# One written order for units 16 to 127, seven products from unit 20 on, and a new plan for the first batch

## The chip, the cores and the metric

The kernel runs on one core of one Trainium2 chip. The core has five engines that matter here, and the rows of the profile name them so: PE (TensorE, with PEld for its weight loads), DVE (VectorE), ACT (ScalarE), POOL (GpSimd) and SP (SyncE, which here only issues DMAs). The metric is the device time of one execution in microseconds (us); lower is better.

## The reference

An attention with a few global tokens, then a two-layer network with a leaky activation:

```python
# batch 8, heads 8, local length 512, global length 32, head size 64, window 32
s_ll = scale * q_l @ k_l^T, masked to |i - j| <= 32
a_l  = softmax(concat[scale * q_l @ k_g^T, s_ll])
out_l = a_l @ concat[v_g, v_l]
out_g = softmax(scale * q_g @ concat[k_g, k_l]^T) @ concat[v_g, v_l]
x = concat[out_g, out_l] as (8 * 544, 512)
h = x @ w_in                      # 512 x 2048
g = max(h, 0) + alpha * min(h, 0) # alpha per hidden column
return g @ w_out                  # 2048 x 512
```

All of it is fp32.

## The kernel before, in words

**Units.** The network is cut into 144 units. Unit T = 16 G + f takes token group G (groups 0 to 7 are the 512 local tokens of a batch, group 8 all 256 global tokens) and hidden block f of 128 columns. A unit has a first layer (`f1`, tile `h_ps`), the activation (tiles `g`, then `gh` and `gl`), and a second layer (`f2`, tiles `o0` to `o3`, shown as `o`) that adds into four banks over the 16 units of a group. The second layer of a unit runs LAG = 2 units after its first layer.

**Three matmuls for one.** An fp32 number is held as an upper part of fewer bits and the rest (`xh` and `xl`, `gh` and `gl`, two halves of `wt`). A product of two such numbers takes three matmuls: upper by upper, rest of the weight by upper, upper by rest. A plain first layer of a unit is so 4 x 3 = 12 matmuls of 512 columns, and a second layer 12 more.

**Seven products.** `f1_fast` takes the first layers of two units (an even one and the odd one after it) together, as a 2 x 2 matrix of blocks by the seven-product scheme. Each product is 6 matmuls of 256 columns: four products (24 matmuls) in the even unit and three (18) in the odd one, 42 against the 24 of 512 columns that two plain first layers take. It needs sums of weights (`weight_sums(q)` for pair q of hidden blocks, tiles `wsum`, `s24`, `s3`), sums of x (`x_sums`, tiles named `b11` to `t4`) and, behind the products, five additions on VectorE (tiles `u` and `h_ps`).

**Activation.** `prelu` is two VectorE instructions that read `h_ps`. The other form, `negatives` on ScalarE and then `add_slopes` on VectorE, has one. In the seven-product units the last pair of a group uses the second form (functions `added` and `both`), the others the first (`even` and `odd`).

**Attention.** It goes in pairs P = 0 to 31 of two heads (four per batch): scores (`s_ps`), softmax, global scores (`g_ps`), values (`o_ps`). The probabilities of P >= 4 go through DRAM to be transposed (`scratch`, `pt`). The pairs of batch G + 1 run in the units of batch G, four units to a pair.

**What sets the order.** Units 0 to 15, with the decoding of all 32 weight tiles (`wraw`, `wt`, `wr`) and attention pairs 0 to 8, stand in an order that the class `Plan` makes in `begin`: each operation has an engine, a cost, its needs and a due time, and `LIST` holds the numbers, with a bias per kind of operation. Its names are `S`, `G`, `T`, `V` (scores, global scores, transposes, values of a pair), `fx`, `fy`, `f1` (first layer of a unit, units 0 and 1 in parts), `fa` and `fb` (second layer by `gh` and by `gl`), `red` (the reduction of scores), `p` (activation), `su` and `d1` to `d3` (weight decoding). Units 16 to 29 (`slow_unit`) are plain, and a list scheduler orders all engines but TensorE there; TensorE runs in the order of the program everywhere. Units 30 and 31 (`border_units`) and 32 to 127 (`fast_unit`, set by `FAST`) stand as written. Units 16, 23 and 30 (`CATCH`) hold two attention steps instead of one. Weight sums are made in units 18 to 29 for q = 0 to 6 and in 33 and 35 for q = 7. SyncE's DMAs are put in order by the list scheduler behind `begin`.

## Time and profile before

| what | value |
|---|---|
| three runs | 884.85, 886.47, 890.36 us (median 886.47) |
| the profiled execution, its own time | 887.61 us |
| its span (first to last instruction) | 885.8 us |
| PE, share of the span | 98% |
| DVE | 70% |
| ACT | 44% |
| POOL | 37% |

The time of an execution is its span and what lies around it, here 1.8 us. A share is a mean over stages with different limits: the first 150 us are not like the rest.

### The profile page before, as it was taken

What the parts mean: (1) busy time and instruction counts of PE and PEld (TensorE: products, weight loads), DVE (VectorE), ACT (ScalarE), POOL (GpSimd) and SP (SyncE); (2) the same over time, 40 slices, a digit from 0 to 9 for tenths busy, and PEclk for the clock granted to TensorE, in tenths of its full rate; (3) what the DMA queues carried; (4) which work ended last, traced back from release to release, by engine and by line L of the source; (5) the groups of instructions that cost most, each with busy time, mean ns of one, the idle gap of its engine ahead of it and who ended that gap; (6) DMA issues with size and microseconds to landing.
All of it is one profiled execution on the core that took longest, in us unless ns stands there. A gap on an engine that the chain in (4) does not pass through costs nothing.

```text
span 885.8 us, 22467 instructions
## 1 busy us (share of the span) xinstructions
PE 866.2 (98%) x8678; PEld 751.2 (85%) x8678; DVE 616.3 (70%) x1690; ACT 392.7 (44%) x1162; POOL 323.9 (37%) x281
## 2 busy tenths in 40 slices
PE   7799999999999999999999999999999999999998
PEld 5677777878888888888898888888898898889898
DVE  7999999976767667666676667666676656455432
ACT  7898885544444334432354334432354324211221
POOL 4455443655434332423243332423243323222222
PEclk9999999999999999999999999999999999999999
DMA  9879997977457766776657666776657553645630
GB/s 357 343 256 387 335 336 251 324 247 236 152 180 220 250 214 220 263 241 232 211 173 254 211 215 217 255 250 231 212 184 250 173 185 95 215 168 169 220 134 25
DMA packets 80906, 201.23 MB, mean 227 GB/s; under 512 B 21280, under 2 KB 41248, under 8 KB 77088
## 3 DMA queue, kind: packets, MB, share of 16 engines
q1 hardware_dynamic: 80800, 199.80, 66.1%
q8 instruction: 69, 1.13, 0.5%
q14 instruction: 37, 0.30, 0.1%
HBM read 160.96 MB, written 38.80 MB: 226 GB/s over the span
## 4 chain that ended last, share of the span: by engine, by line
PE 73%; DVE 14%; DMA 6%; ACT 4%; issue 2%; POOL 1%; SPq 1%; DVEq 0%; ACTq 0%; POOLq 0%
PE o L323 34%; PE h_ps L323 30%; PE o_ps L323 4%; PE s_ps L323 3%; DVE wt L294 2%; PE g_ps L323 2%; DVE wsum L294 2%; DVE p L294 2%; DVE g L294 2%; ACT p L294 2%; DVE wraw L294 1%; DMA pt<-scratch 1%; DMA scratch<-p 1%; DMA v<-in_v_dram 1%; DMA wa<-wt 1%
## 5 line engine op out<-in xcount | busy, mean ns | idle before, releaser
L294 POOL TENSOR_TENSOR gl<-g,gh 128x512 fp32r<-128x512 f32 (+1 forms) x128 | 161.4, 1263 | 368.0 <-ACT gh L294 270.4
L323 PE MATMUL o<-gh,wo 128*128 128x512 f32 (+1 forms) x1024 | 244.4, 380 | 0.0
L323 PE MATMUL h_ps<-xh,wt 128*128 128x256 f32 (+1 forms) x1024 | 222.4, 310 | 2.2 <-DVE g L294 1.3
L294 ACT CAST gh<-g 128x512 fp32r<-128x512 f32 (+1 forms) x144 | 85.9, 597 | 289.0 <-DVE g L294 288.3
L323 PEld LDWEIGHTS o<-gh,wo 128*128 128x128 f32 x1024 | 176.7, 188 | 32.1 <-issue 0.4
L323 PEld LDWEIGHTS h_ps<-xh,wt 128*128 128x128 f32 x1024 | 166.2, 188 | 20.5 <-issue 4.0
L323 PE MATMUL h_ps<-xl,wt 128*128 128x256 f32 (+1 forms) x512 | 157.4, 307 | 0.0
L323 PE MATMUL o<-gl,wo 128*128 128x512 f32 (+1 forms) x512 | 131.2, 377 | 0.0
L294 DVE TENSOR_SCALAR g<-h_ps,alpha_sb 128x512 f32<-128x512 f32 (+1 forms) x116 | 82.5, 712 | 39.0 <-PE h_ps L323 33.6
L323 PEld LDWEIGHTS o<-gl,wo 128*128 128x128 f32 x512 | 92.8, 188 | 18.5
L294 POOL TENSOR_TENSOR p<-p,rz 128x512 f32<-128x512 f32 x64 | 70.7, 1121 | 96.2 <-DVE rz L294 93.4
L323 PEld LDWEIGHTS h_ps<-xl,wt 128*128 128x128 f32 x512 | 96.1, 188 | 5.1
L294 DVE TENSOR_TENSOR h_ps<-u,h_ps 128x256 f32<-128x256 f32 x144 | 61.1, 425 | 50.6 <-PE h_ps L323 48.7
L294 ACT ACTIVATE p<-p,mn 128x128 f32<-128x128 f32 x224 | 86.9, 396 | 5.1 <-DVE mn L294 4.9
L323 PE MATMUL h_ps<-xh,s 128*128 128x256 f32 x480 | 88.6, 280 | 0.4 <-DVE h_ps L294 0.2
L294 DVE TENSOR_TENSOR u<-u,h_ps 128x256 f32<-128x256 f32 x96 | 40.3, 420 | 57.0 <-PE h_ps L323 36.7
L323 PEld LDWEIGHTS h_ps<-xh,s 128*128 128x128 f32 x480 | 75.9, 188 | 4.3 <-ACT xe L294 0.7
L294 DVE SCALAR_TENSOR_TENSOR g<-h_ps,g 128x512 f32<-128x512 f32 (+1 forms) x116 | 75.9, 654 | 3.8
L323 PE MATMUL h_ps<-xl,s 128*128 128x256 f32 x240 | 67.1, 279 | 0.0
L294 POOL TENSOR_TENSOR wt<-wt,wr 128x512 int32<-128x512 int32 x32 | 45.4, 1423 | 52.4 <-DVE wt L294 35.0
L323 PEld LDWEIGHTS o_ps<-pt,v 128*64 128x64 f32 x1600 | 49.7, 138 | 8.2 <-issue 2.7
L323 PE MATMUL o_ps<-pt,v 128*64 128x32 f32 (+1 forms) x1600 | 53.5, 223 | 1.7 <-DMA pt<-scratch 1.0
(102 smaller groups left out, 1137.1 us busy)
## 6 DMA issues: line engine op xcount, KB each, us to landing
wo<-wo SPq DMA_DIRECT2D x128, 512.0 KB, 4.3
v<-in_v_dram SPq DMA_DIRECT2D x29, 1024.0 KB, 5.4
qk<-in_qk_dram SPq DMA_DIRECT2D x30, 672.0 KB, 7.0
wraw<-in_w_dram SPq DMA_DIRECT2D x32, 512.0 KB, 8.4
scratch<-p SPq DMA_DIRECT2D x112, 128.0 KB, 2.8
pt<-scratch SPq DMA_DIRECT2D x28, 512.0 KB, 5.7
wo<-wt SPq DMA_DIRECT2D x16, 512.0 KB, 7.1
out_dram<-ost SPq DMA_DIRECT2D x32, 256.0 KB, 3.5
```

The source lines that it names most:

```text
L294: ins = op(*a, **k)
L323: ins = nc.tensor.matmul(*a, **k)
```

## The change

The plan of the first batch gets other numbers: other biases and due times in `LIST`, other first free times of the engines, and TensorE's costs without the 3% that were added (1.25 times up to 27 us in place of 45 us, then 1.0). What it plans is the same set of operations. All units from 16 to 127 go through one function, `unit`, and stand in the order in which they are written; `slow_unit`, `border_units`, `attn`, the double steps and `x_last` are gone. Units 16 to 19 have plain first layers with the `negatives` form (`f1_plain`), and `f1_fast` begins with unit 20 in place of unit 32. Batch 1 takes its x sums from `x_second`, batches 2 to 7 from `x_sums`. Batches 1 and 2 use `added` and `both` in all pairs. Weight sums for q = 2 to 7 stand in units 17 to 28, in two parts each, those for q = 0 and 1 in units 33 to 38; in batch 2 the hidden blocks start at 4 and wrap round (`hidden`), so that blocks 0 to 3 come last there. Attention step s of pair P stands in unit t with t + 20 = 4 P + s (before, from unit 31 on: t + 22).

```diff
 LIST = dict(
-    first=29.416, pace=6.054, pair0=79.515, pair=19.51, slack=2, ...
+    first=29.07, pace=6.054, pair0=88.993, pair=19.315, slack=2, ...
...
-FAST = range(2 * NF, NB * NF)
-CATCH = (16, 23, 30)
+PLAIN = NF + 4
+FIRSTS = {17: 2, 19: 3, 21: 4, 23: 5, 25: 6, 27: 7, 33: 0, 37: 1}
+RESTS = {18: 2, 20: 3, 22: 4, 24: 5, 26: 6, 28: 7, 34: 0, 38: 1}
...
+LATE = 4
...
-        free = dict(PE=5.4, ACT=2.5, DVE=5.0, POOL=4.0, SP=1.2)
-        lock, dma, kind, landed = 0.0, 3.3, None, [0.0] * 8
+        free = dict(PE=4.5, ACT=2.5, DVE=4.2, POOL=3.2, SP=0.7)
+        lock, dma, kind, landed = 0.0, 2.4, None, [0.0] * 8
...
-                cost = cost * (1.25 if t < 45 else 1.03) + (0.15 if kind != o["kind"] else 0.0)
+                cost = cost * (1.25 if t < 27 else 1.0) + (0.12 if kind != o["kind"] else 0.0)
...
+    def x_second(step):
+
+        if step == 0:
+            less(b11, b12, b11)
+            less(b12, b22, b12)
+            upper(1, "t1", b11)
+            upper(1, "t3", b12)
+        if step == 1:
+            xs[1, "b11"], xs[1, "b21"], xs[1, "b22"], xs[1, "t4"] = halves(0, 0), halves(2, 0), halves(2, 1), halves(0, 1)
+            lower(1, "t1", b11, vec)
+            less(b11, b22, b11)
+            upper(1, "t2", b11)
+            lower(1, "t3", b12, vec)
+            less(b21, b21, b11)
+            lower(1, "t2", b11, vec)
+        if step == 2:
+            for c in range(2):
+                act.copy(xs[1, "t4"](0, c), x_raw[:, 2 + c, 0:256])
+                pool.tensor_tensor(xs[1, "t4"](1, c), x_raw[:, 2 + c, 0:256], xs[1, "t4"](0, c).bitcast(F32), op=ALU.subtract)
...
+    def hidden(T):
+
+        G, f = divmod(T, NF)
+        return (f + LATE) % NF if G == 2 else f
...
-        if f == NF - 1:
+        if f == NF - 1 or G in (1, 2):
             return added, both
         return even, odd
+
+    def f1_plain(T):
+        h = f1(T, True)
+
+        def half():
+            us["below"] = negatives(h)
+
+        def whole():
+            g = us.pop("below")
+            add_slopes(T, g, h)
+            upper_g(T, g, SL)
+            lower_g(T, g, SL)
+
+        return half, whole
...
-    def fast_unit(t):
-        P, s = divmod(steps[t][0], 4)
+    def unit(t):
+        P, s = divmod(t + 20, 4)
...
-        one, two = f1_fast(t)
+        one, two = f1_plain(t) if t < PLAIN else f1_fast(t)
...
+            if t in FIRSTS:
+                late[FIRSTS[t]] = weight_sums(FIRSTS[t], True)
...
+        if t in RESTS and s == 2:
+            late.pop(RESTS[t])()
...
-        pin[0] = t in FAST or t in (2 * NF - 2, 2 * NF - 1)
+        pin[0] = t < NB * NF
```

The first place is TensorE in the first batch, where the second layer begins. `s_ps` are the scores of attention pair 5 (`S5`), the `h_ps` ahead of it end the first layer of unit 2, `gh` and `gl` are the activation of unit 0. Before:

```order
L323 MATMUL h_ps<-xh,wt 128x512 x2
L323 MATMUL h_ps<-xl,wt 128x512
L323 MATMUL s_ps<-qk 32x128 x32
L323 MATMUL o_1003<-gh,wt 128x512 x2
L323 MATMUL o_1004<-gh,wt 128x512 x2
L323 MATMUL o_1005<-gh,wt 128x512 x2
L323 MATMUL o_1006<-gh,wt 128x512 x2
L323 MATMUL h_ps<-xh,wt 128x512 x2
```

Now:

```order
L322 MATMUL h_ps<-xl,wt 128x512
L322 MATMUL o_942<-gh,wt 128x512 x2
L322 MATMUL o_943<-gh,wt 128x512 x2
L322 MATMUL o_944<-gh,wt 128x512 x2
L322 MATMUL o_945<-gh,wt 128x512 x2
L626 MATMUL pt<-consts,sg_sb 128x128 x3
L322 MATMUL o_942<-gl,wt 128x512
L322 MATMUL o_943<-gl,wt 128x512
L322 MATMUL o_944<-gl,wt 128x512
L322 MATMUL o_945<-gl,wt 128x512
L322 MATMUL s_ps<-qk 32x128 x32
```

Second-layer work moved ahead of the scores of pair 5. Further on, the second layer of one unit more, or its `fa` or `fb` part, stands ahead of the values of pairs 4 to 6 (`V4` now follows `fb2`, before `fb1`) and `fa` of one unit more ahead of the first layers of units 9 to 12; ahead of unit 14 and between `V7` and `G8` there is less (`V7 fb11 G8` in place of `V7 fa12 G8`). Ahead of `S4` one quarter of unit 1's first layer (`fy1`, three matmuls) came in, and on VectorE `p0` now stands between the two halves of pair 4's reduction (`red4.0`, `red4.1`) instead of behind both.

The second place is TensorE at units 20 and 21 of batch 1 (the numbers tell the buffers apart: `h_ps_2665` and `h_ps_2666` are the two banks of one pair). Before, unit 20:

```order
L323 MATMUL h_ps_2713<-xh_1235,wt_1210 128x512 x2
L323 MATMUL h_ps_2713<-xl_1236,wt_1210 128x512
L323 MATMUL h_ps_2713<-xh_1553,wt_1210 128x512 x2
L323 MATMUL h_ps_2713<-xl_1554,wt_1210 128x512
L323 MATMUL h_ps_2713<-xh_1871,wt_1210 128x512 x2
L323 MATMUL h_ps_2713<-xl_1872,wt_1210 128x512
L323 MATMUL h_ps_2713<-xh_2209,wt_1210 128x512 x2
L323 MATMUL h_ps_2713<-xl_2210,wt_1210 128x512
```

Now, the last three of its four products:

```order
L322 MATMUL h_ps_2665<-xh_2379,wt_1199 128x256 x2
L322 MATMUL h_ps_2665<-xl_2380,wt_1199 128x256
L322 MATMUL h_ps_2665<-xh_2379,wt_1199 128x256 x2
L322 MATMUL h_ps_2665<-xl_2380,wt_1199 128x256
L322 MATMUL h_ps_2666<-xh_2427,s24_2567 128x256 x2
L322 MATMUL h_ps_2666<-xl_2428,s24_2567 128x256
L322 MATMUL h_ps_2666<-xh_2427,s24_2567 128x256 x2
L322 MATMUL h_ps_2666<-xl_2428,s24_2567 128x256
L322 MATMUL h_ps_2666<-xh_2382,s3_2568 128x256 x2
L322 MATMUL h_ps_2666<-xl_2383,s3_2568 128x256
```

The plain first layer of 512 columns became half-width products, which take both banks and read weight sums (`s24`, `s3`) and x sums.

The third place is VectorE in units 16 to 18. `g` with `alpha_sb` or `beta_sb` is the activation, `x_raw` and `xl` without `o_ps` are the x sums, `gm`, `gz`, `p`, `rz` and `x_glb` belong to attention. Before:

```order
L294 TENSOR_SCALAR g<-h_ps,alpha_sb 128x512
L294 TENSOR_TENSOR wsum<-wt 128x512 x2
L294 SCALAR_TENSOR_TENSOR g<-h_ps,g 128x512
L294 RECIPROCAL rz<-rz 128x4 x2
L294 TENSOR_TENSOR wsum<-wsum 128x256 x4
L294 STREAM_TRANSPOSE p<-p 128x512 x2
```

Now:

```order
L293 SCALAR_TENSOR_TENSOR g<-g,beta_sb,h_ps 128x512
L293 TENSOR_TENSOR x_raw<-x_raw 128x2x256 x2
L293 RECIPROCAL rz<-rz 128x4 x2
L293 SCALAR_TENSOR_TENSOR g<-g,beta_sb,h_ps 128x512
L293 TENSOR_TENSOR xl<-x_raw,xh 128x512
L293 TENSOR_TENSOR x_raw<-x_raw 128x2x256
L293 TENSOR_TENSOR xl<-x_raw,xh 128x512
L293 TENSOR_TENSOR x_raw<-x_raw 128x2x256
L293 TENSOR_TENSOR xl<-x_raw,xh 128x512
L293 STREAM_TRANSPOSE p<-p 128x512 x2
L293 TENSOR_TENSOR wsum<-wt 128x512 x2
```

The activation has one VectorE instruction for two, the sums of x came in, and the weight sums moved behind them.

## Rows read from the trace of the kernel before

**Rows 1.** The page: the span, and busy time, share and number of instructions of each engine.

```profile
span 885.8 us, 22467 instructions
...
PE 866.2 (98%) x8678; PEld 751.2 (85%) x8678; DVE 616.3 (70%) x1690; ACT 392.7 (44%) x1162; POOL 323.9 (37%) x281
```

**Rows 2.** Stretches of the span: its bounds and length, then busy time and number of instructions of PE, PEld, DVE, ACT and POOL, the granted PE clock, the DMA engines' busy share and GB/s.

```profile
0.00:20.00 20.00, 15.52 (x349) 10.48 (x349) 14.90 (x58) 13.85 (x62) 10.06 (x23) 1.00 0.92 352
20.00:35.00 15.00, 10.57 (x185) 8.75 (x186) 14.24 (x46) 13.16 (x39) 9.09 (x9) 1.00 1.02 416
35.00:60.00 25.00, 22.71 (x274) 17.57 (x273) 23.85 (x74) 21.27 (x53) 10.76 (x8) 1.00 0.68 230
60.00:90.00 30.00, 28.99 (x301) 22.99 (x300) 29.24 (x82) 26.78 (x75) 16.58 (x12) 1.00 0.96 363
90.00:151.44 61.44, 59.03 (x547) 45.88 (x543) 60.05 (x152) 46.78 (x114) 27.23 (x21) 1.00 0.89 311
151.44:180.00 28.56, 28.56 (x246) 23.25 (x242) 28.15 (x63) 13.07 (x40) 16.96 (x15) 1.00 0.93 332
180.00:297.00 117.00, 115.88 (x1160) 96.71 (x1159) 81.89 (x251) 50.71 (x168) 52.13 (x46) 1.00 0.66 213
297.00:720.00 423.00, 423.00 (x4465) 376.16 (x4464) 285.09 (x830) 170.47 (x541) 137.79 (x110) 1.00 0.67 222
```

**Rows 3.** The chain of work that ended last, in order of time: start, length, what. Plain units (before 230 us) and seven-product units (from 299 us).

```profile
204.43 2.75 PE o L323 x12
207.17 2.75 PE h_ps L323 x12
...
299.90 2.12 PE h_ps L323 x18
302.02 2.75 PE o L323 x12
304.76 2.82 PE h_ps L323 x24
```

**Rows 4.** TensorE in order of time in the first batch, the instructions that waited: start, length, line, operation, tiles, shape, count, and in brackets the idle time before and what ended it.

```profile
41.56 0.38 PE L323 MATMUL s_ps<-qk 64*32 64x128 f32 x2 [1.05 <-DVE xl L294]
42.41 1.13 PE L323 MATMUL s_ps<-qk 64*32 64x128 f32 x62 [0.48 <-DVE xl L294]
...
46.90 0.73 PE L323 MATMUL h_ps<-xh,wt 128*128 128x512 f32 x2 [0.76 <-DVE g L294]
...
63.42 1.59 PE L323 MATMUL o_ps<-pt,v 128*64 128x32 f32 x48 [1.01 <-DMA pt<-scratch]
...
96.94 0.50 PE L323 MATMUL h_ps<-xh,wt 128*128 128x512 f32 x1 [0.70 <-DVE wt L294]
...
118.87 0.50 PE L323 MATMUL h_ps<-xh,wt 128*128 128x512 f32 x1 [0.20 <-DVE wt L294]
...
136.77 0.70 PE L323 MATMUL g_ps<-qk 128*64 128x288 f32 x6 [0.48 <-ACT x_raw L294]
```

**Rows 5.** The same view where batch 2 begins and where the last attention pair is done.

```profile
284.02 0.69 PE L323 MATMUL g_ps<-pt,v 128*64 128x32 f32 x16 [0.69 <-DVE g_ps L294]
...
745.22 0.48 PE L323 MATMUL h_ps<-xh,s 128*128 128x256 f32 x2 [0.25 <-DVE h_ps L294]
```

**Rows 6.** VectorE in order of time at 46 us: the last piece of the reduction of a pair's scores, and the activation of unit 0 behind it.

```profile
45.86 0.31 DVE L294 CUSTOM_DVE_ANT_0 p<-s_ps,mask 128x128 f32<-128x128 f32 x1
...
46.07 0.77 DVE L294 SCALAR_TENSOR_TENSOR g<-g,beta_sb,h_ps 128x512 f32<-128x512 f32 x1
```

**Rows 7.** All engines in order of time where unit 47, the last of batch 2, ends: the two additions into the banks, the ScalarE part of the activation, its VectorE part, and the first matmul of unit 48.

```profile
351.17 0.41 DVE L294 TENSOR_TENSOR h_ps<-u,h_ps 128x256 f32<-128x256 f32 x1
...
351.61 0.60 ACT L294 ACTIVATE g<-h_ps 128x512 f32<-128x512 f32 x1 [1.07 <-DVE h_ps L294]
351.64 2.00 PE L323 MATMUL o<-gh,wo 128*128 128x512 f32 x8
351.84 0.43 DVE L294 TENSOR_TENSOR h_ps<-u,h_ps 128x256 f32<-128x256 f32 x1 [0.26 <-PE h_ps L323]
...
352.78 1.40 DVE L294 SCALAR_TENSOR_TENSOR g<-g,beta_sb,h_ps 128x512 f32<-128x512 f32 x2
...
354.39 0.40 PE L323 MATMUL h_ps<-xh,wt 128*128 128x256 f32 x2
```

**Rows 8.** VectorE's instructions by group and shape from 300 to 640 us: count, busy us and mean ns of one, idle time before.

```profile
L294 DVE TENSOR_SCALAR g<-h_ps,alpha_sb 128x512 f32<-128x512 f32 x49 | 36.8, 751 | 2.7
L294 DVE TENSOR_TENSOR h_ps<-u,h_ps 128x256 f32<-128x256 f32 x83 | 35.3, 425 | 20.4 <-PE h_ps L323 19.3
L294 DVE SCALAR_TENSOR_TENSOR g<-h_ps,g 128x512 f32<-128x512 f32 x49 | 33.9, 692 | 1.7
...
L294 DVE SCALAR_TENSOR_TENSOR g<-g,beta_sb,h_ps 128x512 f32<-128x512 f32 x6 | 4.2, 741 | 0.0
```

**Rows 9.** Weight sums on VectorE in order of time, and GpSimd at the same time.

```profile
156.49 1.35 DVE L294 TENSOR_TENSOR wsum<-wsum 128x256 f32<-128x256 f32 x3
...
161.92 4.17 DVE L294 TENSOR_TENSOR wsum<-wsum 128x256 f32<-128x256 f32 x4
...
162.01 2.37 POOL L294 TENSOR_TENSOR p<-p,rz 128x512 f32<-128x512 f32 x2 [0.16 <-DVE rz L294]
164.35 1.46 POOL L294 TENSOR_TENSOR gl<-g,gh 128x512 fp32r<-128x512 f32 x1
```

More of the change, by code (lines that the diff above doesn't have):

```diff
@@ L794, in prepare @@
             G += 1
-        if G == NB - 1 and (f, at) in LAST_STEPS:
-            x_last(LAST_STEPS.index((f, at)))
-        if G * NF not in FAST or (f, at) not in X_STEPS:
-            return
-        if G < NB - 1:
+        if 2 <= G < NB and (f, at) in X_STEPS:
             x_sums(G, X_STEPS.index((f, at)))
@@ L827, in product @@
             for j, e in ((0, 0), (1, 0), (0, 1)):
-                matmul(dst, w[:, j, 128 * c : 128 * c + 128], x[e][:, 256 * c : 256 * c + 256], start=start, stop=not start, skip_group_check=True)
+                piece = x(e, c) if callable(x) else x[e][:, 256 * c : 256 * c + 256]
+                matmul(dst, w[:, j, 128 * c : 128 * c + 128], piece, start=start, stop=not start, skip_group_check=True)
                 start = False
+    def hidden(T):
+        G, f = divmod(T, NF)
+        return (f + LATE) % NF if G == 2 else f
     def f1_fast(T):
         G, f = divmod(T, NF)
-        q = f // 2
+        q = hidden(T) // 2
         x = lambda name: xs[G, name]
@@ L892, in add_slopes @@
     def add_slopes(T, g, h):
-        f = T % NF
+        f = hidden(T)
         vec.scalar_tensor_tensor(g, g, beta_sb[:, f : f + 1], h, op0=ALU.mult, op1=ALU.add)
@@ L903, in slopes @@
     def slopes(T, h, n):
-        f = T % NF
+        f = hidden(T)
         g = stage("g")
@@ L977, in longformer_ffn @@
     gpart = {}
-    def values(P, first):
-        last = gpart.pop(P)
-        if live(P - 1):
-            ob = bank(first, "o_ps")
-            pv_all(P - 1, ob, last)
-        if live(P):
-            global_scores(P)
-        if live(P - 1):
-            pv_out(P - 1, ob, last)
     def values_pe(P):
@@ L1151, in longformer_ffn @@
-    tails = []
     begin()
     pin_sync[0] = False
-    steps = [[] for t in range(NT + LAG)]
-    u = NPRE + NF
-    for t in range(NF, NT + LAG):
-        steps[t] = [u, u + 1] if t in CATCH else [u]
-        u = steps[t][-1] + 1
-    def attention(t, at):
-        with tc.high_priority(offset=HP):
-            if len(steps[t]) == 1:
-                attn(steps[t][0], at)
-                return
-            order = [(k, a) for k in range(2) for a in ("pre", "mid", "post")]
-            i = 2 * ("pre", "mid", "post").index(at)
-            for k, a in order[i : i + 2]:
-                attn(steps[t][k], a)
@@ L1236, in fast_unit @@
             two()
+            if t == NF:
+                x_second(0)
+            if t == PLAIN:
+                x_second(2)
+            if t in RESTS and s == 0:
+                late.pop(RESTS[t])()
             prepare(t, "mid")
@@ L1264, in fast_unit @@
         f2(t - LAG, 1)
+        if t in RESTS and s == 2:
+            late.pop(RESTS[t])()
+    late = {}
     load_out_weights(NF)
```

164 lines of the change are left out of this document (29 added, 135 removed).

## The prediction

> **What bounds the kernel now.** I read the page first, then the stretches, then the chain, then the waits of the stretch that is not full. The page says that PE is busy 98% of the span and no other engine over 70% (VectorE; PEld is TensorE's own weight load) [rows 1]. The stretches say where the other 2% are [rows 2]. From 297 to 720 us PE is busy 423.0 of 423.0 us: nothing but less matmul work makes this part shorter. From 151.44 (where the second layer of unit 14 begins) to 297 it is idle 1.1 us in 145.6, though VectorE has 35.5 us free there. Before 151.44 it is idle 14.6 us: 4.5 up to 20 us, 4.4 up to 35, 2.3 up to 60, 1.0 up to 90, 2.4 after. In that first stretch TensorE does not stand alone: from 60 to 151.44 VectorE is busy 89.3 of 91.4 us, from 35 to 60 23.9 of 25. So the first batch has two full engines, and whatever is won on TensorE there by order has to be paid out of 3.3 us of free VectorE time between 35 and 151 us. The granted clock is 1.00 in every stretch, the higher of the two levels (2.4 GHz), so no term comes from it.
>
> **The change, part by part.** The sum goes against the profiled execution, 887.61 us, which is 1.1 above the median of the three runs; I take the 1.1 off at the end.
>
> *Seven products for units 20 to 31.* The chain has the lengths of whole first layers [rows 3]. A plain one is 12 matmuls in 2.75 us, so a pair takes 5.50. With seven products the even unit is 24 matmuls in 2.82 and the odd one 18 in 2.12, together 4.94. That is 0.56 less per pair, on an engine that has no gap there; six pairs more are changed: -3.3 us (3.36). The attention work and the second layers of batches 1 to 7 stay the same in number.
>
> The Trainium skill has a rule against this term: "TensorE: Matmul & The Clock Gate", section "Back-to-back issue gap", gives about 81 ns per matmul of 128 columns and 131 ns for 512 in a stream with weight loads. An estimate between these for 256 columns is 98 ns; a pair would then be 24 x 131 = 3.1 us plain and 42 x 98 = 4.1 us with seven products, and the change would cost 1 us per pair, 5.8 in all. The trace disagrees on both: 2.75 / 12 = 229 ns and 2.12 / 18 = 118 ns [rows 3]. The measurement decides.
>
> *What the seven products ask of the others.* VectorE's price per pair goes by its own rows [rows 8]: before, two plain units took 2 x (0.75 + 0.69) = 2.9 us; now 5 x 0.43 + 2 x 0.74 = 3.6. The x sums of batch 1 come in addition, seven instructions in units 16 and 17, and nothing reads them before unit 20, over 16 us of matmuls later (three units of 5.5). Against this, the plain units 16 to 19 and all of batch 2 use the form with one VectorE instruction. The ScalarE part of that form falls on an engine that is busy 64 of 145.6 us there [rows 2]. I cost all of this at nothing, because VectorE has 35.5 us free in the stretch that takes it; if it comes in the wrong order it costs waits, which is the rival below.
>
> The one place where this form could stop TensorE is the release of the banks between two pairs. It exists already in unit 47, the last of its batch [rows 7]: the first layer ends at 351.64, the VectorE part begins at 352.78, its first half frees the first bank at 353.48, and unit 48 begins at 354.39 with no wait. The slack is 0.9 us, without scores between the pairs.
>
> *Stalls after the first batch.* Those of before are 1.1 us (to 297) and 0.25 at 745.22, where the last x sums are made [rows 2, 5]. The waits for scores and values at the change of schemes go with the old units 30 to 35; the last attention pair comes two units later and the last x sums go through the common function. New waits can come at units 20, 24 and 28, whose weight sums are finished only two units ahead. Bounds: -1.4 and, from the worst old single wait of 0.69 at each of these three and at the end of batch 6, +2.8. I take -0.5, nearer to the old state, since VectorE is no fuller than it was.
>
> *The first batch.* No operation is added or removed; only the order changes. I go through the waits that I can name [rows 4]. `S4` waits 1.05 + 0.48 us for VectorE; `fy1`, three matmuls, 0.69 us by a plain quarter, now fills part: -0.69. Unit 2's first layer waits 0.76 for `p0`, which stood behind the whole reduction of pair 4 [rows 6]; four of its eight pieces, 0.21 us apart, now come after it: -0.76. `V4` waits 1.01 for the fetch of the probabilities; a whole second layer (2.75) more stands ahead: -1.01. Units 9 and 12 wait 0.70 and 0.20 for weights; an upper half (1.83 us, 8 of 12 matmuls of 2.75) more stands ahead of each: -0.90. Against these, `G8` waits 0.48 for a copy behind `V7` with 1.83 us of cover, and now has 0.92: +0.9. Together -2.5. Earlier, up to 35 us, the order on TensorE is nearly the old one (`G1` moved ahead of `S2`, `G4` ahead of `Tg3`), and ScalarE is busy 27 of 35 us [rows 2]; I take 0 there. VectorE gives part of the gain back, since it is full from 60 us on: what TensorE no longer waits for in one place it will ask for sooner in the next. I take -2.0. Bounds: the gain ends at the 10.1 us that PE is idle between 20 and 151.44, or, with VectorE's 3.3 us as the limit after 35, at 4.4 + 3.3 = 7.7; the loss, if the order is worse where I see nothing, at the same named waits a second time, 4.7 with that of `G8`.
>
> *With one answer.* Which hidden block comes when in batch 2, the order of the stores of weights (the same DMAs of the same size, on SyncE, whose order behind the first batch is still found by the scheduler), the new first free times: they change no engine's work, and I cost them at 0. Where they need cover it is TensorE's queue of two units; DMA is busy 0.66 of the time from 180 to 297 and 0.93 before that, so a late output weight could show only between 151 and 180.
>
> Sum: 887.61 - 3.3 - 0.5 - 2.0 = 881.8 for the profiled execution, and 880.7 for the median of runs like the three shown: 0.65% less.
>
> **The rivals.**
>
> *VectorE is the limit of the first batch, and the order wins nothing there.* For it: 89.3 of 91.4 us busy. Against it: the waits named above are in TensorE's own queue, and some (the fetch) are not VectorE's. It leaves the term of the products alone: 887.6 - 3.3 - 0.5 = 883.8, median 882.7.
>
> *The order wins much more.* For it: 8.9 us of idle TensorE before 35 us, which I valued at 0. Against it: ScalarE and VectorE are nearly as full there. With the 7.7 us of the bound: 887.6 - 3.3 - 0.5 - 7.7 = 876.1, median 875.0.
>
> *Slower: the written order puts VectorE's sums ahead of what TensorE waits for.* VectorE takes its instructions in order, and now the scheduler no longer moves weight sums out of the way. A weight sum is six instructions with both inputs in SBUF. Three of them took 1.35 us alone, and four took 4.17 beside GpSimd's work of 162.01 to 165.81 [rows 9], so 0.59 more each and 3.5 for six. Queued behind it are the additions into the banks, and the next pair on TensorE waits for these. With 0.9 us of slack taken off, 2.6 remain; eight weight sums, six in batch 1 and two in batch 2, make 21 at most. With half of that, 10.5, the time is 892.3, median 891.2. It decides from 0.7 us per sum beyond the slack (5.8 / 8); below that the kernel still gains. Against it: the same contention stood in batch 1 before, and PE was idle 0.0 us from 151 to 180 beside it. The Trainium skill ("SBUF — State Buffer", section "SBUF: two separate sides") says that such a VectorE instruction and a GpSimd one hold the shared ports one at a time, the whole instruction long; the trace agrees with 4.17 against 1.8 us.
>
> *Half-width matmuls are not half as long in batch 1*, so that the change doesn't do what it says. They would have to take 5.50 / 42 = 131 ns and not 118 to win nothing. PEld is busy 376 of 423 us where they run now, so weight loads have 11% left [rows 2], and the same weights and shapes are used. It would give 885.1, median 884.0.
>
> **How the numbers follow.** Chances: my forecast 0.63 (own range 877.5 to 884), VectorE as the limit 0.18, much more 0.10, slower 0.07, no shorter products 0.02. The range goes from 875.5, past most of the second rival, to 887, past the first and the last, and leaves out the slower one and the end of the large gain. A measurement of this kernel can tell about 1% from no change, 8.9 us of 886.5, so the bounds are 877.6 and 895.3. Faster by over 1%: 0.10 and 0.08 of my own case, 0.18. Slower by over 1%: only the upper part of the slower rival, whose middle is 891.2, and what I have not thought of, 0.05. Within 1%: 0.77.
>
> **What would show it.** Right: `h_ps` groups of 24 and 18 matmuls of 256 columns from unit 20 on, 2.82 and 2.12 us long; two units of batch 1 without attention in 10.4 us (4.94 and twice 2.75) instead of 11.0; the second layer of unit 14 beginning some 2 us before 151.4; PE idle under 1.5 us from there to the end of the attention. Wrong: a first batch that is as long as before, waits of `h_ps` for VectorE at the even units 20 to 46, or waits of `o` for the load of `wo` between 150 and 190 us.

## The result, and the profile after

The change makes the kernel 0.7% slower. The changed kernel takes 893.34 us (median of 8 runs, 890.67 to 894.70), the kernel before 886.81 us beside it (8 runs); the ratio is 1.0069, 95% interval 1.0052 to 1.0087. I had forecast 880.7 us with a range up to 887.0. The profiled execution took 891.17 us, with a span of 889.4 us, 3.6 more than before [rows 1].

The stretches of the changed kernel, with columns as in [rows 2]; the first begins where the second layer of unit 14 does:

```profile
149.97:180.00 30.03, 27.52 (x242) 22.59 (x241) 21.33 (x67) 15.67 (x46) 11.02 (x9) 0.94 0.75 269
180.00:270.00 90.00, 86.81 (x894) 76.33 (x892) 69.70 (x186) 49.76 (x148) 46.44 (x41) 1.00 0.57 189
270.00:297.00 27.00, 27.00 (x320) 24.02 (x317) 17.46 (x53) 12.69 (x38) 10.23 (x9) 1.00 0.70 241
297.00:720.00 423.00, 419.61 (x4466) 371.27 (x4466) 282.23 (x841) 175.57 (x554) 137.09 (x113) 1.00 0.66 222
```

The part that had been full, 297 to 720 us, now has 3.4 us of idle TensorE; the part from 150 to 270 us has 5.7, and there the granted clock is below 1.00 for the first time. What TensorE waited for, in total, times and longest, from 149 to 297 us and from 297 to 720 us:

```profile
PE g_ps L322 <- DVE g_ps L293: 4.6, 4, 2.5
PE h_ps L322 <- POOL xl L293: 0.8, 1, 0.8
PE h_ps L322 <- DVE g L293: 0.3, 1, 0.3
...
PE h_ps L322 <- POOL xl L293: 3.4, 4, 0.9
```

Neither of these two waits is on my list. **The first** stands in the values blocks of units 18, 22, 26 and 30. TensorE and then VectorE in order of time in unit 18 of the changed kernel:

```profile
161.06 1.59 PE L322 MATMUL o_ps<-pt,v 128*64 128x32 f32 x48
165.16 0.80 PE L322 MATMUL g_ps<-pt,v 128*64 128x32 f32 x16 [2.51 <-DVE g_ps L293]
...
166.84 3.09 PE L322 MATMUL o<-gh,wo 128*128 128x512 f32 x8
...
161.33 0.68 DVE L293 TENSOR_TENSOR x_raw<-x_raw 128x512 f32<-128x512 f32 x1
161.94 0.68 DVE L293 TENSOR_TENSOR xl<-x_raw,xh 128x512 fp32r<-128x512 f32 x1
162.54 1.29 DVE L293 STREAM_TRANSPOSE p<-p 128x512 f32<-128x512 f32 x2
163.76 1.25 DVE L293 TENSOR_TENSOR wsum<-wt 128x512 f32<-128x512 f32 x2
164.97 0.72 DVE L293 SCALAR_TENSOR_TENSOR g<-g,beta_sb,h_ps 128x512 f32<-128x512 f32 x1
165.02 0.09 DVE L293 MEMSET g_ps<- 64x32 f32 x1
```

TensorE needs a bank of which VectorE first has to clear a part (0.09 us). The clearing reads nothing, but it stands behind the x sums, the transposes and the weight sums of unit 17; in units 22 and 26 it stands behind weight sums of 2.4 us, in unit 30 behind x sums of 2.3 us. From 165 to 170 us the granted clock is 0.66, a mean of the two levels (1.00 is 2.4 GHz, 0.50 is 1.2): the eight matmuls behind the wait take 3.09 us, not 2.00.

**The second** stands at the first odd unit of batches 2 to 7. Rows of all engines, in order of time, from the border of batch 4 (units 64 and 65) of the changed kernel; those between them are left out:

```profile
460.01 0.68 DVE L293 TENSOR_TENSOR xl<-x_raw,xh 128x512 fp32r<-128x512 f32 x1
460.65 0.40 PE L322 MATMUL h_ps<-xh,s 128*128 128x256 f32 x2
460.73 0.69 DVE L293 TENSOR_TENSOR x_raw<-x_raw 128x512 f32<-128x512 f32 x1
461.45 0.62 ACT L293 CAST xh<-x_raw 128x512 fp32r<-128x512 f32 x1 [0.62 <-DVE x_raw L293]
462.15 1.27 POOL L293 TENSOR_TENSOR xl<-x_raw,xh 128x512 fp32r<-128x512 f32 x1 [2.58 <-ACT xh L293]
463.48 0.38 PE L322 MATMUL h_ps<-xl,wt 128*128 128x256 f32 x1 [0.84 <-POOL xl L293]
464.04 0.39 PE L322 MATMUL o<-gh,wo 128*128 128x512 f32 x1
```

This first layer takes 464.04 - 460.65 = 3.39 us where 2.12 was the price [rows 3]. It reads the x sum t4, which goes from VectorE over ScalarE to GpSimd only now. Over the six borders this is 7.2 us (1.35, 1.33, 1.26, 1.28, 1.33, 0.68).

The same border in the kernel before (the first layer of the even unit begins, GpSimd makes t4's lower half, the first layer of the odd unit begins), and behind the dots the start of the even unit's first layer in the changed kernel:

```profile
453.96 0.40 PE L323 MATMUL h_ps<-xh,wt 128*128 128x256 f32 x2
460.73 1.29 POOL L294 TENSOR_TENSOR xl<-x_raw,xh 128x512 fp32r<-128x512 f32 x1 [2.28 <-ACT xh L294]
462.24 0.40 PE L323 MATMUL h_ps<-xh,s 128*128 128x256 f32 x2
...
454.96 0.51 PE L322 MATMUL h_ps<-xh,wt 128*128 128x256 f32 x2
```

Counted from the start of the even unit's first layer, t4 is done after 8.1 us there (462.02) and after 8.5 here (463.42): hardly later. But the odd unit's first layer begins after 8.3 us there and after 5.7 here. The values block of 2.5 us that lay between the two first layers is gone from this place; scores ahead of the even unit have come instead.

The sum from the two traces, from the start of the second layer of unit 14 to that of unit 128: 691.2 us before, 696.2 after, so + 5.0 behind a first batch that ends 1.5 us sooner (149.97, not 151.44). In it: the borders + 7.2; the g_ps waits 4.6, and 1.7 for the matmuls at the low clock (the values block from 165.16 on 1.68 us, not 1.10, the second layer behind it 3.84, not 2.75); the rest, with the seven products, is 8.5 less.

### The profile page after: what moved, and what is told of

It reads as the page before. It is cut to its first block, busy times and chain, and to the rows that moved or that the text cites. A ratio compares the mean times of both kernels' runs of the same rounds, so it can differ in the third digit from the quotient of the medians.

```text
span 889.4 us, 22789 instructions
## 1 busy us (share of the span) xinstructions
PE 863.4 (97%) x8786; PEld 752.5 (85%) x8786; DVE 614.3 (69%) x1703; ACT 414.4 (47%) x1203; POOL 321.8 (36%) x283
## 4 chain that ended last, share of the span: by engine, by line
PE 69%; DVE 12%; issue 7%; POOL 5%; DMA 3%; ACT 3%; SPq 0%; POOLq 0%; DVEq 0%; ACTq 0%
PE o L322 32%; PE h_ps L322 28%; PE o_ps L322 3%; PE s_ps L322 3%; PE g_ps L322 3%; DVE wt L293 2%; POOL gl L293 2%; DVE g L293 2%; DVE p L293 2%; POOL xl L293 2%; DVE wraw L293 1%; DMA scratch<-p 1%; DVE xl L293 1%; DVE mn L293 1%; DMA wa<-wt 1%
## 5 line engine op out<-in xcount | busy, mean ns | idle before, releaser
L322 PE MATMUL h_ps<-xh,wt 128*128 128x256 f32 (+1 forms) x1024 | 210.4, 300 | 4.2 <-DVE g L293 2.7
L322 PE MATMUL h_ps<-xl,wt 128*128 128x256 f32 (+1 forms) x512 | 152.0, 297 | 4.7 <-POOL xl L293 4.7
L293 DVE TENSOR_TENSOR h_ps<-u,h_ps 128x256 f32<-128x256 f32 x162 | 68.0, 425 | 58.4 <-PE h_ps L322 56.2
L322 PE MATMUL h_ps<-xh,s 128*128 128x256 f32 x552 | 100.1, 278 | 0.0
L322 PEld LDWEIGHTS h_ps<-xh,s 128*128 128x128 f32 x552 | 87.0, 188 | 3.8
L293 DVE TENSOR_SCALAR g<-h_ps,alpha_sb 128x512 f32<-128x512 f32 (+1 forms) x86 | 60.3, 702 | 35.5 <-PE h_ps L322 31.7
L293 DVE TENSOR_TENSOR u<-u,h_ps 128x256 f32<-128x256 f32 x108 | 45.3, 420 | 55.2 <-PE h_ps L322 51.6
L322 PE MATMUL h_ps<-xl,s 128*128 128x256 f32 x276 | 76.6, 278 | 0.0
L293 DVE CUSTOM_DVE_ANT_0 p<-s_ps,mask 128x128 f32<-128x128 f32 x224 | 49.7, 284 | 14.1 <-PE s_ps L322 12.1
L293 DVE SCALAR_TENSOR_TENSOR g<-h_ps,g 128x512 f32<-128x512 f32 (+1 forms) x86 | 55.2, 642 | 3.0
```

Source lines behind the costliest of these rows:

```text
L293: ins = op(*a, **k)
L322: ins = nc.tensor.matmul(*a, **k)
```

## The experiments

Each run stood beside the kernel before on the same chip, and ratios are to that; not all runs were on one chip. My theory (A): two waits, each the result of an order on VectorE. The rival (B): batch 1 and the borders have more VectorE work than fits, and whatever is moved, something else is late.

**Clearing g_ps one unit earlier.**

```diff
-        if s == 2 and (live(P) or live(P - 1)):
+        if s == 1 and (live(P) or live(P - 1)):
             gpart[P] = global_bank(P)
```

> The changed kernel, with one thing moved: the clearing of the bank of the global scores (g_ps, 0.09 us on VectorE) is written one unit earlier, at the start of the odd unit with s = 1, ahead of that unit's x sums and weight sums. In the trace of the changed kernel the values blocks of units 18, 22, 26 and 30 wait 4.6 us in all for this clearing, which stands in VectorE's order behind weight sums and x sums; in the first of them (2.51 us) TensorE's granted clock falls, and the second layer behind it takes 3.84 instead of 2.75 us. Theory A (the wait is only one of order): the waits of g_ps go, the clock stays at 1.00, and the time falls by 4.6 + 1.1 = 5.7, from 893.3 to about 887.6; the waits at the starts of batches 2 to 7 stay. Rival B (VectorE has too much work in batch 1, the order matters little): TensorE then waits about as long for the next thing that VectorE is late with, the additions into the banks and the slopes of batch 1, and the time stays within 1.5 us of 893.3.

Measured: 890.57 us (886.51 to 893.69), ratio 1.0055 (1.0034 to 1.0076). The median lies between the two expectations, 2.8 us under the changed kernel's on another chip. The trace, which is of the fastest of the six executions, is clear: no wait of g_ps is left behind unit 14, the clock is 1.00, and units 14 to 30 take 102.5 us, not 107.5, though one wait of 1.4 us at unit 30 is new. From the second layer of unit 14 to that of unit 128 it is 690.5 us, not 696.2: the 5.7 of theory A. The pair of runs that differ only in this edit on one chip, further down, gives 1.0065 to 1.0006, 5.2 us. Theory A for this wait; why the median here shows only half of it is open.

**The second layer ahead at the borders.**

```diff
+        border = f == 1 and t > 2 * NF
+        if border:
+            f2(t - LAG, 0)
         one, two = f1_plain(t) if t < PLAIN else f1_fast(t)
...
-        f2(t - LAG, 0)
+        if not border:
+            f2(t - LAG, 0)
```

> The changed kernel, with another order on TensorE alone at six places: in units 33, 49, 65, 81, 97 and 113 (the first odd unit of batches 2 to 7) the upper eight matmuls of the second layer that follows (1.83 us) are placed ahead of the first layer of the unit, whose last product reads the x sum t4. In the trace of the changed kernel this first layer takes 3.4 us instead of 2.1 in five of these units and 2.8 in the sixth, 7.2 us in all, with waits for the lower half of t4 on GpSimd. Theory A (t4 comes late since the unit before it now holds scores and no values block): 1.83 us of cover is more than the 1.3 us that are missing, so all of it goes, and the time falls by about 7, from 893.3 to 886.2. Rival B (the sum of many small waits of VectorE is the cause, and the border only one place where they show): PE is then idle elsewhere in the same batch, in the next pair that waits for a bank, and the time falls by less than 2 us.

Measured: 892.90 us, ratio 1.0089 (1.0076 to 1.0102): nothing won, as the rival said. VectorE and TensorE behind the first layer of unit 49 in this run:

```profile
365.51 0.43 DVE L293 TENSOR_TENSOR h_ps<-u,h_ps 128x256 f32<-128x256 f32 x1 [2.49 <-PE h_ps L322]
365.97 0.75 DVE L293 TENSOR_SCALAR g<-h_ps,alpha_sb 128x512 f32<-128x512 f32 x1
366.76 0.69 DVE L293 SCALAR_TENSOR_TENSOR g<-h_ps,g 128x512 f32<-128x512 f32 x1
...
367.60 0.47 PE L322 MATMUL h_ps<-xh,wt 128*128 128x256 f32 x2 [0.49 <-DVE g L293]
```

The first layer now takes 2.12 us, but the next pair waits for its banks, which VectorE frees in 1.9 us at the earliest, and the 1.83 us of matmuls that covered this have gone ahead. It waits for the second bank too, and takes 3.4 us instead of 2.9. The cover can be used once.

**Both.**

> Both edits: the clearing of g_ps one unit earlier, and the eight upper matmuls ahead of the first layer at the six borders. Theory A (two separate waits, both of order): the gains add up, 893.3 - 5.7 - 7.2 = 880.4, which would be faster than the kernel before by 6.4 us (0.7%), of which 3.4 are the seven products and 1.5 the first batch. Rival B (VectorE's work as such): 890 or more.

Measured: 887.50 us, ratio 1.0022 (1.0011 to 1.0032), between the two expectations. Its profiled execution has the span of the clearing alone, 884.7 us, and the borders take as long in sum as ever; that its median is 3 us lower than that of the clearing alone, whose runs spread over 7 us, I can't explain.

**The plan of the first batch alone, in the kernel before.** Its biases, due times, costs and first free times; no code.

> The kernel before, with the changed kernel's plan of the first batch alone: its biases and due times, its costs and its first free times; the units from 16 on are those of before. If the new plan by itself wins what the two traces show (the second layer of unit 14 begins 1.5 us earlier), the time is 886.8 - 1.5 = 885.3. If the gain comes from how the first batch meets units 16 and on, or is given back there, it is 886.8 or more. Had my prediction's term been right, it would be 884.8.

Measured: 886.92 us, ratio 1.0016 (1.0004 to 1.0027): 1.4 us slower, not 2.0 faster. TensorE in that trace, and the stretch behind (columns as above):

```profile
148.83 0.73 PE L323 MATMUL h_ps<-xh,wt 128*128 128x512 f32 x2 [1.90 <-DVE g L294]
...
150.00:155.00 5.00, 5.00 (x75) 3.69 (x74) 5.00 (x9) 1.14 (x2) 0.50 (x1) 0.69 1.05 382
```

Late in the batch TensorE waits 1.90 us for the slopes of a unit on VectorE, and the clock falls behind it too. The second layer of unit 14 begins at 154.5 us in this trace, 3 us later than before.

**The changed kernel once more.**

> The changed kernel itself, unedited, as the base of this call's comparisons on the same chip. Both theories: 1.0069 times the kernel before, 891.5 to 893.5; in its trace again four waits of g_ps in batch 1 and six first layers that are 0.7 to 1.3 us too long at the starts of the batches.

Measured: 897.18 us, ratio 1.0103 (1.0079 to 1.0127); the g_ps waits (4.5 us, four) and the borders are there again. The ratio is not the 1.0069 of the first chip, nor inside its interval: for one and the same kernel, ratios on two chips lie 3 us apart. The two traces agree to 0.1 us behind unit 14 (696.1 and 696.2 us to unit 128).

**An earlier t4.**

```diff
         if step == 5:
             upper(G, "b22", b22)
             lower(G, "b22", b22, pool)
+            less(b12, b21, b11)
             upper(G, "b21", b21)
+            lower(G, "b21", b21, pool)
+            upper(G, "t4", b12)
         if step == 6:
-            lower(G, "b21", b21, vec)
-            less(b21, b21, b11)
-            upper(G, "t4", b21)
-            lower(G, "t4", b21, pool)
+            lower(G, "t4", b12, vec)
```

> The changed kernel with the x sum t4 of batches 2 to 7 made earlier: it is written over b12, which is no longer needed then, one step sooner, its upper half is made on ScalarE ahead of the scores' exponentials, its lower half on VectorE and not on GpSimd, and GpSimd makes the lower half of b21 instead. The same number of operations, and the order of TensorE as in the changed kernel. The run with the second layer placed ahead had shown that the first layers at the borders no longer wait for t4, but that the next pair then waits for its banks, since the slopes on VectorE need that second layer as their cover. Here the cover stays. Theory A (t4 is late by order alone): the six first layers take 2.1 us again, 7.2 us in all; the time falls by 6 to 7.2 from the base. Rival B (VectorE is too full at the border, with scores, sums and slopes in a row): its sums for u come 0.7 us later and the odd unit's first product waits for them instead; the time falls by less than 3.

Measured: 893.54 us, ratio 1.0065 (1.0043 to 1.0087). In medians this is 3.6 us less than the base, between the two expectations; in the traces nothing is won (696.9 us from unit 14 to 128, 696.1 in the base), so the 3.6 stay unexplained. The borders are as long as before (6.15 to 6.35 us from one second layer to the next at five of them, not 4.88), but what TensorE waits for is another thing, as the rival said. The next run has the same border.

**The earlier t4 with the earlier clearing.**

> The earlier t4 and the earlier clearing of g_ps together. Theory A: base - 7 - 4 to 5.7 = 880 to 882, which is 4 to 5 us faster than the kernel before, near what my sum had said. Rival B: 886 or more.

Measured: 887.52 us, ratio 1.0006 (0.9988 to 1.0025): the rival's 886 or more, though the wait of g_ps is gone. VectorE, GpSimd and TensorE at the same border:

```profile
448.37 1.41 DVE L293 SCALAR_TENSOR_TENSOR g<-g,beta_sb,h_ps 128x512 f32<-128x512 f32 x2 [0.34 <-ACT g L293]
449.88 2.41 DVE L293 TENSOR_TENSOR xl<-x_raw,xh 128x512 fp32r<-128x512 f32 x2
452.33 1.67 DVE L293 TENSOR_TENSOR x_raw<-x_raw 128x512 f32<-128x512 f32 x1
...
455.60 0.87 DVE L293 TENSOR_TENSOR u<-u,h_ps 128x256 f32<-128x256 f32 x2
456.50 0.43 DVE L293 TENSOR_TENSOR h_ps<-u,h_ps 128x256 f32<-128x256 f32 x1
...
450.44 3.00 POOL L293 TENSOR_TENSOR gl<-g,gh 128x512 fp32r<-128x512 f32 x2 [11.89 <-ACT gh L293]
...
457.08 0.47 PE L322 MATMUL h_ps<-xh,s 128*128 128x256 f32 x2 [1.04 <-DVE h_ps L293]
```

VectorE works 8.5 us on end, from the slopes over the x sums and the scores (the dots) to the additions behind the products (`u`, then `h_ps`), the last of which ends 1 us too late. The rival is right about the border: time, not order alone. Part of it is slow: the subtraction takes 1.67 us beside GpSimd's work, and 0.69 without it. The Trainium skill ("SBUF — State Buffer", section "SBUF: two separate sides") says of such VectorE and GpSimd instructions that they hold the shared ports one at a time; the rows agree.

**The seven products undone.** Plain units up to 31, weight sums behind their units, no x sums for batch 1.

> The same two edits, and the seven products of units 20 to 31 undone: batch 1 is plain to its end, the seven VectorE subtractions and the halves of the x sums of batch 1 are left out, the weight sums follow their units as in the kernel before (sums of pair q in units 19 + 2q and 20 + 2q), and batch 2 takes the hidden blocks in their plain order. Against the run with the two edits alone this measures the term of the products by itself. If the term of my sum is right: + 3.4 us. If the sums of batch 1 on VectorE cost TensorE as much as the products save: 0 or less.

Measured: 897.02 us, ratio 1.0112 (1.0087 to 1.0137), 9.4 us slower than the run above. The + 3.4 fails as a sum, since only part of it is the products: waits of 1.9 and 3.2 us in units 32 and 33, where x sums and weight sums now meet, are in it, and so is the clock of 0.66 behind them. Between the second layers of units 20 and 26, where neither trace has a wait of that kind, three pairs take 38.38 us, and 36.76 with seven products: 0.54 per pair. My term had 0.56.

**The attention steps moved back.** Unit 24 makes scores and values; behind it step s of pair P lies where 4 P + s = t + 22.

```diff
-        P, s = divmod(t + 20, 4)
+        P, s = divmod(t + (20 if t <= SHIFT else 22), 4)
+        double = t == SHIFT
```

> The changed kernel with the earlier clearing of g_ps, and the attention steps moved back to where they stood before: in unit 24 the scores of pair 11 and the values of pair 10 come in the same unit, and from unit 25 on step s of pair P lies in the unit t with t + 22 = 4 P + s, as in the kernel before (the change had made it t + 20). The first unit of each batch then has a values block and no scores: its 2.6 us on TensorE lie between the two first layers of the pair, and VectorE has no reduction of scores (1.7 us) among the x sums. The run with t4 made earlier had the wait of 1.0 us at the same border move from t4 to VectorE's sums, so that place is short of VectorE time, not of order alone. Theory A2 (the place of the attention steps sets the wait at the borders): the six waits go without any change of the x sums; the time falls by 7 from that of the earlier clearing alone, whose profiled execution took 886.5 us, to 879.5 in a like run; the double unit 24 costs 0 to 1.5. Rival B2 (the x sums in the common function are too late wherever the attention stands): the waits stay at 0.8 or more each and the time falls by less than 2.

Measured: 893.07 us, ratio 1.0074 (1.0058 to 1.0090). TensorE in unit 24; and VectorE in unit 63 and TensorE in unit 64, the first of batch 4:

```profile
203.50 0.31 PE L323 MATMUL o_ps<-pt,v 128*64 128x32 f32 x4 [1.03 <-issue]
205.61 2.43 PE L323 MATMUL o_ps<-pt,v 128*64 128x64 f32 x44 [1.80 <-DMA pt<-scratch]
...
451.27 1.86 DVE L294 TENSOR_TENSOR x_raw<-x_raw 128x256 f32<-128x256 f32 x2
...
453.31 0.76 DVE L294 TENSOR_TENSOR h_ps<-u,h_ps 128x256 f32<-128x256 f32 x2
...
455.36 0.48 PE L323 MATMUL h_ps<-xh,wt 128*128 128x256 f32 x2 [0.48 <-DVE g L294]
...
458.44 0.38 PE L323 MATMUL h_ps<-xl,s 128*128 128x256 f32 x1 [0.48 <-DVE xl L294]
```

The odd unit no longer waits (4.99 us from one second layer to the next, as before). But the even unit does, for a bank and for an x sum: the change's own spread of the x sums, made for values that come late, puts two subtractions (1.86 us) ahead of the additions into the banks. (The change rewrote `x_sums` too: it makes the first subtraction a step later, the second in two halves, and the third a step sooner.) A batch takes 100.3 us, against 100.2 in the changed kernel. Neither expectation held: with the old place the odd unit's wait goes, and others of about the same sum come. I read this as the place of the attention and the spread of the x sums belonging together; no run of the changed kernel has the old spread, so that is not shown. The double unit waits for its probabilities besides.

**The old plan of the first batch, with the steps moved back and without.**

> As the run with the steps moved back, and the first batch by the plan of the kernel before: its biases, due times, costs and free times. The plan of the change, put alone into the kernel before, had cost 1.4 us there (interval 0.4 to 2.4) where I had predicted a gain of 2.0. If the new plan is worse by itself, this run is 1 to 2 us faster than the run with the steps moved back; if it is only worse where it meets the old units 16 and on, this run is 1.5 us slower than that.

> The changed kernel with the earlier clearing of g_ps and the first batch by the plan of the kernel before; the attention steps stay where the change put them. Against the run with the steps moved back and the old plan, it gives the price of the borders a second time: 7 us slower by theory A2, under 2 by rival B2. Against the run with the earlier clearing alone it gives the first batch: 1 to 2 faster if the new plan is worse by itself.

Measured: 892.31 us, ratio 1.0073 (1.0061 to 1.0085), no difference from the new plan; and 889.29, ratio 1.0033 (1.0018 to 1.0047), against 1.0055 with the new one on another chip. The run that leaves the steps where the change put them is 3.0 us faster than the one with the steps moved back, on one chip and with one plan: both theories had it slower.

**The kernel before once more.**

> The kernel before itself, for a second trace of its first batch. In its first trace the second layer of unit 14 begins at 151.4 us; in the traces so far with the changed plan it begins at 149.7 to 152.0, once at 153.4 and once at 154.5. If the plan of the change is faster by the 1.5 us of the first pair of traces, this one begins at 151 to 152 again; if that pair was a matter of chance, it lies between 149.7 and 151.

Measured: 885.53 us, one run. The second layer of unit 14 begins at 151.50, as expected if the plan were faster. But with the new plan it begins anywhere from 149.7 to 153.4 us in the twelve traces of changed kernels (151.1 in the mean), and at 154.5 in the kernel before; with the old plan at 150.9 to 152.4 in six (151.8 in the mean). The 149.97 of the first trace lies near the low end of this; the means are 0.7 us apart, so about half of the 1.5 us was luck.

**The lower half of t3 on GpSimd.** In step 4, and the same with another order in unit 28, with the new and the old plan:

```diff
-            lower(G, "t3", b12, vec)
+            lower(G, "t3", b12, pool)
         if step == 5:
```

> The changed kernel with the earlier clearing of g_ps, the earlier t4, and one more thing: the lower half of the x sum t3 of batches 2 to 7 is made on GpSimd and not on VectorE. In the trace of the run with the first two edits, VectorE is busy without a gap from 448.4 to 456.9 us, and the odd unit waits 1.0 us for its sums for u; of this, two lower halves took 2.41 us and the subtraction for t4 1.67 instead of 0.69, both beside GpSimd. GpSimd was idle from 442 to 450.4. Theory A3 (the border is short of about 1 us of VectorE time, and only there): without the 0.7 us and its share of the slowing the sums for u end before the odd unit asks for them; the six waits go, and the time falls by 5 to 7 from 887.5, to 880.5 to 882.5. Rival B3 (GpSimd then slows the rest of VectorE's work by as much, or its own lower halves of b22 and b21 come too late): the odd unit waits for GpSimd instead and the time falls by less than 2.

> The same, and in unit 28 the first x sums of batch 2 are written ahead of the second part of the weight sums of pair 7. In the runs with the earlier clearing the next pair waits 1.1 to 1.4 us there, since the x sum on VectorE waits 1.8 us for its upper half, which stands on ScalarE behind that of the weight sums. If that is order alone: 1 us less than the run without this. If the weight sums then come late for unit 30 or its successors: no change.

> The same as the run with the order of unit 28 changed, but with the first batch by the plan of the kernel before. If the plan of the change is worth the 2.0 us of my sum, this run is 2 us slower; by the runs so far (0.4 to 2.4 us slower when the new plan was put into the kernel before; 2 us apart in the same direction in the changed kernel with the earlier clearing) it is 0 to 2 us faster.

Measured: 898.39, 902.26 and 900.92 us, ratios 1.0156 (1.0142 to 1.0170), 1.0197 and 1.0183. GpSimd and TensorE in the first of them:

```profile
454.68 2.54 POOL L293 TENSOR_TENSOR gl<-g,gh 128x512 fp32r<-128x512 f32 x2 [11.76 <-ACT gh L293]
457.19 4.22 POOL L293 TENSOR_TENSOR xl<-x_raw,xh 128x512 fp32r<-128x512 f32 x3
...
458.50 0.38 PE L322 MATMUL h_ps<-xl,s 128*128 128x256 f32 x1 [1.55 <-POOL xl L293]
```

My own mistake, of the same kind as the change's: the even unit reads t3, and I had put it behind the lower halves of g. The other order in unit 28 does not win its 1 us either: that run is 3.9 us slower, and the first unit of batch 2 waits 2.4 us for GpSimd instead of 1.6.

**The same, ahead of them.**

```diff
             upper(G, "t3", b12)
+            lower(G, "t3", b12, pool)
             upper(G, "t2", b11)
         if step == 4:
             lower(G, "t2", b11, vec)
-            lower(G, "t3", b12, vec)
```

> As the run with the lower half of t3 on GpSimd, but issued one step earlier, in unit 15 of the batch before, right behind its upper half and ahead of the lower halves of g, where GpSimd had been idle for 11.8 us. By the trace of the earlier run it would begin at 453.5 and end at 454.8, 2 us before the even unit asks for it at 456.6; the subtraction for t4 behind it on VectorE then begins 3.6 us sooner than there (454.9, not 458.5), and 1 us sooner than in the run with the first two edits, counted from the start of the even unit. Theory A3 (the border lacks about 1 us of VectorE time and nothing else): the wait of 1.0 us for the sums for u goes at all six borders; base of the first two edits (ratio to the kernel before 1.0006) less 5 to 6.5 us: ratio 0.993 to 0.995. Rival B3 (whatever is moved, the next engine in the chain is late there): ratio 0.999 or more.

> The same with the first batch by the plan of the kernel before. By the pairs so far (with the earlier clearing alone the old plan was 2 us faster; with the steps moved back it made no difference; in the run with the t3 on GpSimd 1.3 us faster) it is 0 to 2 us faster than the run with the new plan; if the plan is worth what my sum says, 2 us slower.

Measured: 882.55 us, ratio 0.9949 (0.9933 to 0.9965), and with the old plan 882.09, ratio 0.9946 (0.9931 to 0.9960). What TensorE waits for in the first of them from 297 to 846 us, all of it, and GpSimd at the border:

```profile
PE h_ps L322 <- POOL xe L293: 0.2, 1, 0.2
...
448.95 1.28 POOL L293 TENSOR_TENSOR xl<-x_raw,xh 128x512 fp32r<-128x512 f32 x1 [10.72 <-ACT xh L293]
450.19 3.46 POOL L293 TENSOR_TENSOR gl<-g,gh 128x512 fp32r<-128x512 f32 x2
```

The borders take 5.2 us from one second layer to the next, not 6.2. Theory A3 held: the place lacked about 1 us of VectorE, GpSimd had been idle for 10.7 us beside it, and one instruction per border given to it sooner is worth 5.1 us (1.0006 to 0.9949, on two chips) and 5.3 us in the traces. The slow subtraction stays, with 1.78 us beside GpSimd; what left VectorE is one lower half of 1.1 us. With three edits the change is faster than the kernel before by 0.5%, near what its products had promised: 880.8 us of span against 885.8 and 883.7 in the two traces of the kernel before. A wait of 1.4 us at unit 30 is still in it.

Medians hold the first batch, which varies, and come from several chips. The traces without the first batch, from the start of the second layer of unit 14 to that of unit 128, repeat better (0.1 and 2.2 us apart for one kernel) and tell the two causes apart:

| kernel | us |
|---|---|
| before, two traces | 691.2, 689.0 |
| changed, two traces | 696.2, 696.1 |
| second layer ahead at the borders | 696.4 |
| earlier t4 | 696.9 |
| earlier clearing | 690.5 |
| earlier clearing and second layer ahead | 690.5 |
| earlier clearing and earlier t4 | 691.1 |
| these two, and t3 on GpSimd early | 685.8 |

## Why the prediction was wrong

- **Seven products, - 3.3: right.** 0.54 us per pair measured, and first layers of 2.81 to 2.94 and 2.04 to 2.13 us in batch 1. An estimate from the figures of the Trainium skill ("TensorE: Matmul & The Clock Gate", section "Back-to-back issue gap") had each pair 1 us dearer; these rows speak against it again.
- **"I cost all of this at nothing, because VectorE has 35.5 us free in the stretch": this step failed.** The free time of 145 us says nothing of the 3 us in which a values block waits. It cost 4.6 us and, in this trace, 1.7 of low clock. I had looked for late work among what TensorE reads (weight sums, additions); what was late is a clearing of 0.09 us that reads nothing and that a written order can put behind anything. The same wait was in front of me, once: the 0.69 us at 284.02 in [rows 5] is TensorE waiting for this clearing behind weight sums, as VectorE's rows in the kernel before show. I took its length for a bound and did not ask for its cause.

```profile
281.21 2.60 DVE L294 TENSOR_TENSOR wsum<-wsum 128x256 f32<-128x256 f32 x4
283.88 0.09 DVE L294 MEMSET g_ps<- 64x32 f32 x1
```

- **"Stalls after the first batch", - 0.5 with + 2.8 as its upper bound: mis-sized, this step failed too.** Together the g_ps waits, the low clock and the borders are + 13.5. I read "the last attention pair comes two units later" as an event at the end of the attention. It holds in every batch: the last pair's values now come in the 15th unit and not in the 13th, and scores stand at the border, so the odd unit comes 2.6 us sooner for t4 (5.7 us behind the even one, not 8.3) and VectorE has more work there, six times. And my bound was the worst old wait; waits that one order has leave no bound for another.
- **The rival "slower" (0.07)** had the mechanism, VectorE's sums ahead of what TensorE waits for, but in the wrong place (the additions into the banks of units 20 to 46), without the borders, and with too small a chance. That its 891.2 us lies near the 893.3 measured is luck. A change that takes the scheduler away from VectorE's whole queue deserved more.
- **The first batch, - 2.0:** not shown. Of the waits that I named, those of `S4`, `V4` and `G8` are gone, the last against my + 0.9. That of unit 2 for `p0` grew from 0.76 to 1.50 us where I had taken it off; those for weights moved from units 9 and 12 to 5, 8 and 11 and grew from 0.90 to 1.5. TensorE's waits from 20 to 150 us fall from 10.1 to 8.2 us in the one trace, and 1.5 us of that reach unit 14. In medians the new plan never wins: 1.4 slower in the kernel before, 0 to 2 slower in four pairs of the changed one, though the intervals of each pair overlap. Which of its waits make it vary is open.

## What to carry to other kernels

When an order is written out by hand, go through every wait of the engine that is full and ask what stands ahead of its releaser in the releaser's queue, the smallest instructions first; an average of free time over a long stretch answers nothing. When a step is shifted in a loop that has a border, lay out the engines' work for the few units around the border: who has which us there, and what arrives later than before. A wait that only moves when its cause is moved is short of time on that engine; look for an engine that is idle just before, and give it an instruction that nobody waits behind.

## What was not expected of the hardware

- **Two rates of the same matmul.** In the first trace of the kernel before, 79 of 82 first layers with seven products (up to unit 113) run at about 118 ns per matmul of 256 columns; in the second trace, of the same program, 35 of 82 run at about 113. The rate mostly changes at a block of scores or at a stall and holds until the next; in units 114 to 127, without attention, it changes from unit to unit in nearly every trace. Between the two traces it is worth 2.1 us (286.9 and 284.8 us for all first layers between the second layers of units 14 and 128). The changed kernel's trace has the shorter one in 44 of 94 first layers, so by an estimate from these counts some 2.7 of its 8.5 us (2.1 x 41 / 32) come from it. The first trace of the kernel before is the odd one: the other traces have 22 to 48 of 94, or 35, 36 and 45 of 82, so this is a slow base and no gain of the change. I found no cause.
- **A wait of TensorE can cost more than its length, and its length does not tell whether.** Behind the 2.51 us in unit 18 the granted clock was 0.66 over the next 5 us, 1.7 us on top of the wait. The same wait in other traces was followed by 0.50 (second layer ahead at the borders) and by 1.00 (earlier t4, where the eight matmuls behind it took 2.11 us). Behind 1.2 us at 30 us, in the three traces of changed kernels with the old plan that have this wait, it was 0.66; behind 1.6 us, with t3 on GpSimd, 1.00. So part of the spread between executions of one kernel can be the clock; no run separates it.
